# Decode attention with a squared-ReLU MLP: K transposed on VectorE in 32 by 32 blocks, scores as 16 full-width products per unit

## The chip, the cores and the metric

The kernel runs on one core of a Trainium2 chip. The metric is the device time of one execution in microseconds, 134.0 before the change (median of three runs, 133.91 to 134.0). The engines are named as in the profile: PE (TensorE), DVE (VectorE), ACT (ScalarE), POOL (GpSimd) and SP (SyncE, which here only issues transfers).

## The reference

One decode step for two batch rows of width 576: a layer norm, then an attention over the last 2048 cached positions and a two-layer MLP, both fed by the normalized row, and a sum of all three. There are 32 query heads and 16 key/value heads of 128 elements, so two query heads share one K and one V.

```python
W = min(4096, max(256, Sk // 4))                     # 2048 of 8192 positions
q = (xn @ wq).reshape(B, 1, 32, 128)
k = repeat(k_cache[:, :, Sk - W:, :], 2, axis=1)     # the same for v
p = softmax(einsum("bhqd,bhkd->bhqk", q, k) * 128 ** -0.5)
a = einsum("bhqk,bhkd->bhqd", p, v).reshape(B, 1, 4096) @ wo
h = relu(xn @ w1 + b1)
out = x + a + (h * h) @ w2 + b2                      # B = 2, w1 is 576 x 4608
```

All inputs are bfloat16. Nearly all the bytes are the K and V windows, 16.8 MB each, and the weights wq, wo, w1 and w2.

## The kernel before

**Units.** The 16 K/V heads times 2 batch rows are worked in 8 units of 4 heads of one batch row. A unit's K is one transfer of 2 MB into a tile of 128 partitions (4 heads times 32 runs of positions) by 8192 elements (64 positions of 128); V has the same form. `load_k(u)` and `load_v(u)` issue them on SP's queue; both take buffers from one pool of six. The large weights wq, w1 and wo follow each other in a single buffer (`issue_flat`), so each waits until the one before has been used up. The order of the 24 large transfers is written out by hand: k0, wq, k1, v0, k2, v1, k3, then one V and one K per unit, w1 between v5 and k7, and wo and the pieces of w2 at the end.

**The K transposes.** The scores need K with the head dimension on the partitions. `transposes(u, g)` (L258), called eight times a unit, has PE turn four 128 by 128 blocks of 4-byte pairs (two neighbouring bfloat16 elements count as one pair) into a PSUM tile `kT_ps`, and then copies that tile to `kT` in SBUF: on ACT for even g (L270), on DVE for odd g (L272).

**The scores.** `scores(u, t)` (L274) works on half a unit. Its stationary tile is a slice of `qz`, 128 by 32, with the query values of the unit's heads at their places and zeros elsewhere; four such products, one per column group of the array, run side by side, so a unit takes 16 products of 32 columns by 512. A product with `far_h` first puts a large negative number wherever row and head do not belong together. `qz` is made once, in `q_block` (L226), from the query product q_ps by way of copies (L238), transposes and copies (L254).

**The softmax.** `softmax(u)` (L288) takes the row maximum (L291) and a masked form of it (L293) on DVE, the maximum over all partitions on POOL (`partition_all_reduce`, gmax, L295), the bias on DVE (gown, L298), the exponential on ACT (L302), and turns the result in 32 by 32 blocks on DVE (pT, L305).

**The values.** `pv(u)` (L314) multiplies pT with V into o_ps, `pv_end(u)` (L326) gathers four parts into o1 on DVE, and its `fin` divides by the sum and writes the unit's columns of `ws`. pT and o1 have two buffers each, so the values of unit u-2 are worked in step u. `mlp_h` (L356) makes the hidden row; `out_acc` (L216) adds ws times wo and the hidden row times w2 into one PSUM tile.

**Order.** Matmuls and PE transposes are pinned to the order in which the program names them (`keep_in_program_order`, L93 to L97). All else is placed by a scheduler that reorders the instructions of an engine. The program runs q_block after unit 0's transposes, then one `step(u)` per unit, `mlp_h` before the last step, and the output products at the end.

Of the kernel before, what the change touches and what calls it, by code (L numbers as in the profile page):

```python
# [16 lines left out]
def kernel(  # L17
# [32 lines left out]
    JG = 8  # L50
    NG = NJ // JG
# [5 lines left out]
    TG = NG // NT  # L57
    QZ = 2 * NC
    assert SR == 32 and NG % NT == 0

# [34 lines left out]

    def transpose(*a, **k):
        tc.keep_in_program_order(nc.tensor.transpose(*a, **k))  # L97
# [18 lines left out]
    def issue_flat(w, name):  # L116
        n = w.shape[0] * w.shape[1] // P
        tl = wbig.tile([P, NH * L1], BF16, tag="wbig", name=name)
        nc.sync.dma_start(out=tl[:, 0:n], in_=w.rearrange("r n -> (r n)").rearrange("(p l) -> p l", p=P))
        return tl  # L120

    const.tile([P, 144], F32, name="pad_0")
# [15 lines left out]
    tmp_f = work.tile([P, 2, Dh], F32, tag="tmp", name="tmp_f")  # L138
# [50 lines left out]
    nc.vector.tensor_scalar(out=off[:], in0=own[:], scalar1=BIG, scalar2=-BIG, op0=ALU.mult, op1=ALU.add)  # L189
    of_h = const.tile([P, NC * WC], F32, name="of_h")  # L190
# [29 lines left out]

    qz = const.tile([P, NQ, B, 2, 3 * QZ], BF16, name="qz")
    nc.gpsimd.memset(qz[:], 0.0)
# [3 lines left out]
    def q_block():  # L226
        for t in range(NH):
            for g in range(NG4):
                o = t * LQ + g * QW
                matmul(q_ps[32 * g:32 * g + 2 * B, :], lhsT=xnT[:, t].rearrange("p x b -> p (x b)"),  # L230
                       rhs=wq_sb[:, o:o + QW], start=(t == 0), stop=(t == NH - 1), skip_group_check=True,
                       tile_position=(0, 32 * g))
        row_t = const.tile([RB, 4 * HW], BF16, tag="row", name="qrow")
        qrow = row_t[:, 0:2 * QW]
        nh = QH // 2
        for k in range(2):
            cp = nc.scalar.copy if k else nc.vector.tensor_copy
            cp(out=qrow[:, k * QW:(k + 1) * QW].rearrange("p (i a d) -> p i a d", a=2, d=Dh),  # L238
               in_=q_ps[0:RB, k * QW // 2:(k + 1) * QW // 2].rearrange("p (i d) -> p i d", d=Dh).unsqueeze(2)
               .to_broadcast([RB, nh, 2, Dh]))  # L240
        qrow_f = qrow.bitcast(F32)
        qT_ps = psum.tile([P, QH * P], F32, tag="sc", bufs=2, name="qT_ps")
        for i in range(QH):
            transpose(out=qT_ps[:, i * P:i * P + RB], in_=qrow_f[:, i * Dh:(i + 1) * Dh],
                      identity=ident_f[0:RB, 0:RB])
        qT_v = qT_ps[:].bitcast(BF16).rearrange("p (i g e x b c) -> p b x g c e i", g=NG4 // 2, e=2, x=32 // B, b=B, c=2)
        hd = Dh // 2
        for j2 in range(2):
            cp = nc.scalar.copy if j2 else nc.vector.tensor_copy
            pp = slice(hd * j2, hd * (j2 + 1))  # L250
            o = QZ + NC * j2
            for b in range(B):
                for half in range(2):
                    cp(out=qz[pp, half * NQ // 2:(half + 1) * NQ // 2, b, :, o:o + NC].rearrange(  # L254
                        "p g c (e i) -> p g c e i", e=2), in_=qT_v[pp, b, half])

    kT_tiles, sc_tiles, pT_tiles, o1_tiles, o_tiles = {}, {}, {}, {}, {}
    def transposes(u, g):  # L258
        k_f = k_tiles[u][:].bitcast(F32)
        kT_ps = psum.tile([P, JG * P], BF16, tag="kT", bufs=3, name=f"kT_ps_{u}_{g}")  # L260
        kT_f = kT_ps[:].bitcast(F32)
        for i in range(JG // 2):
            j = g * JG // 2 + i
            transpose(out=kT_f[:, i * P:(i + 1) * P], in_=k_f[:, j * P:(j + 1) * P], identity=ident_f[:])
        t, o = divmod(g, TG)
        if o == 0:
            kT_tiles[(u, t)] = ktpool.tile([P, TG * JG * P], BF16, tag="kT_sb", name=f"kT_{u}_{t}")
        kT = kT_tiles[(u, t)][:, o * JG * P:(o + 1) * JG * P]
        if g % 2 == 0:
            nc.scalar.copy(out=kT, in_=kT_ps[:])  # L270
        else:
            nc.vector.tensor_copy(out=kT, in_=kT_ps[:])  # L272

    def scores(u, t):  # L274
        tq, b = divmod(u, B)
        if t == 0:
            sc_tiles[u] = psum.tile([P, NJJ * 32], F32, tag="sc", bufs=2, name=f"sc_ps_{u}")
            matmul(sc_tiles[u][:], lhsT=far_h[:], rhs=is_h, start=True, stop=False, skip_group_check=True)
        sc_ps = sc_tiles[u]
        kT = kT_tiles.pop((u, t))[:].rearrange("p (j k c) -> p j k c", k=P, c=2)  # L280
        z = QZ * (1 - t)
        for c in range(2):
            for g in range(4):
                matmul(sc_ps[32 * g:32 * (g + 1), :], lhsT=qz[:, tq, b, c, z:z + SR],
                       rhs=kT[:, :, 32 * g:32 * (g + 1), c], start=False, stop=(t == NT - 1 and c == 1),
                       skip_group_check=True, tile_position=(0, 32 * g))

    def softmax(u):  # L288
        sc_ps = sc_tiles.pop(u)
        m1 = work.tile([P, 1], F32, tag="m1", name=f"m1_{u}")  # L290
        nc.vector.tensor_reduce(out=m1[:], in_=sc_ps[:], axis=AX.X, op=ALU.max)  # L291
        m2 = work.tile([P, NC], F32, tag="m2", name=f"m2_{u}")
        nc.vector.tensor_scalar(out=m2[:], in0=off[:], scalar1=m1[:, 0:1], scalar2=None, op0=ALU.add)  # L293
        gmax = work.tile([P, NC], F32, tag="gmax", name=f"gmax_{u}")
        nc.gpsimd.partition_all_reduce(gmax[:], m2[:], channels=P, reduce_op=ReduceOp.max)  # L295
        gown = work.tile([P, NC], F32, tag="gown", name=f"gown_{u}")
        bias = work.tile([P, 1], F32, tag="bias", name=f"bias_{u}")
        nc.vector.scalar_tensor_tensor(out=gown[:], in0=gmax[:], scalar=-scale, in1=own[:], op0=ALU.mult,  # L298
                                       op1=ALU.mult, accum_out=bias[:])
        p_sb = work.tile([P, NJJ * 32], BF16, tag="p_sb", bufs=1, name=f"p_{u}")  # L300
        o1 = keep.tile([P, Dh + 1], F32, tag="o1", name=f"o1_{u}")
        nc.scalar.activation(out=p_sb[:], in_=sc_ps[:], func=ACT.Exp, bias=bias[:, 0:1], scale=scale,  # L302
                             accum_out=o1[:, Dh:Dh + 1])
        pT = keep.tile([P, NJJ, SR], BF16, tag="pT", name=f"pT_{u}")
        nc.vector.transpose(out=pT[:].rearrange("p j r -> p (j r)"), in_=p_sb[:])  # L305
        pT_tiles[u] = pT
        o1_tiles[u] = o1
# [6 lines left out]
    def pv(u, part, parts):  # L314
        n = NJJ // parts
        if part == 0:
            o_tiles[u] = psum.tile([P, NS * Dh], F32, tag="o", name=f"o_ps_{u}")
        v = v_tiles[u][:].rearrange("p (t j s d) -> p j t s d", t=NT, s=2, d=Dh)
        for j in range(part * n, (part + 1) * n):
# [3 lines left out]
        if part == parts - 1:  # L323
            pT_tiles.pop(u)

    def pv_end(u):  # L326
# [3 lines left out]
        for k in range(NS):  # L330
            kw = dict(out=o1[:, 0:Dh], in0=o_ps[:, k * Dh:(k + 1) * Dh])
            if k == 0:
                nc.vector.tensor_scalar(scalar1=in_s[:, 0:1], scalar2=None, op0=ALU.mult, **kw)
            else:
                nc.vector.scalar_tensor_tensor(scalar=in_s[:, k:k + 1], in1=o1[:, 0:Dh], op0=ALU.mult, op1=ALU.add,  # L335
                                               **kw)

        def fin():
# [5 lines left out]
            nc.vector.reciprocal(out=linv[pp, :], in_=op[pp, Dh:Dh + 1])  # L344
            om_t = work.tile([P, Dh], F32, tag="om", name=f"om_{u}")
            om = om_t[pp, :].rearrange("p (q r) -> p q r", r=WR)
            nc.vector.scalar_tensor_tensor(out=om, in0=op[pp, 0:Dh].rearrange("p (q r) -> p q r", r=WR),
                                           scalar=linv[pp, 0:1], op0=ALU.mult, op1=ALU.mult,
                                           in1=own_c[pp, :].unsqueeze(2).to_broadcast([32, WC, WR]))
            with nc.allow_low_precision(reason="sums of one term and zeros"):  # L350
                nc.vector.tensor_reduce(out=ws[pp, :, BS * b], in_=om.rearrange("p q r -> p r q"), axis=AX.X,  # L351
                                        op=ALU.add)
# [3 lines left out]
    def mlp_h(w1_sb):  # L356
        h_ps = [psum.tile([P, HB], F32, tag="kT", bufs=3, name=f"h_ps_{k}") for k in range(2)]
# [29 lines left out]
    def step(u):  # L387
        fin = None
        w = u - 2
        with_pv = w >= 0  # L390
        for g in range(NG):
            transposes(u, g)
            if with_pv and g == 1:
                pv(w, 0, 2)
            if with_pv and g == 2:
                pv(w, 1, 2)
                fin = pv_end(w)
            if g == TG + 1:
                scores(u, 0)
            if g == TG + 2 and fin:  # L400
                fin()
        scores(u, 1)
        softmax(u)

    def pv_all(u):
        pv(u, 0, 1)
        pv_end(u)()

    for g in range(NG):
        transposes(0, g)  # L410
    q_block()
    for t in range(NT):
        scores(0, t)
    softmax(0)
    load_v(2)
    b1_rows = B_b1.rearrange("(x n) -> x n", n=HW)
# [4 lines left out]
    load_k(4)  # L421
# [16 lines left out]
    nc.sync.dma_start(out=w2a_sb[:], in_=w2_rows[0])  # L438
# [49 lines left out]
```

## Time and profile before

| What | Value |
|---|---|
| time, median of three runs | 134.0 us |
| the profiled execution's own time | 133.92 us |
| its span, first to last instruction | 132.1 us |
| PE busy | 84.6 us, 64% |
| DVE busy | 63.2 us, 48% |
| ACT busy | 46.7 us, 35% |
| POOL busy | 4.9 us, 4% |
| loads from memory | 53.6 MB, 406 GB/s over the span |
| mean granted PE clock | 0.834 |

In a line of groups stand the source line, the engine, the operation, output and inputs, shapes and the number of instructions; then the busy time and the mean of one in ns; then the engine's idle time just before them and what ended it. In a line of a timeline stand the start and the duration in us, and in brackets the idle time before. The rows PEclk and DMA have 40 digits, one for each fortieth of the span, in tenths: the granted clock of PE and the busy share of the transfer engines.

### The profile page before, as it was taken

Reading aid. Unit: us, or ns where it says so; the run is one execution under the profiler, and the core shown is the slowest. Engines: PE = TensorE matmul, PEld = TensorE weight load, DVE = VectorE, ACT = ScalarE, POOL = GpSimd, SP = SyncE. Lnnn points to the kernel's source line nnn. Section 1 sums busy time; section 2 is a strip of 40 time slices with the busy share of each in tenths; the row PEclk is TensorE's granted clock in tenths of the full one; section 3 lists DMA queues with packets and bytes.
Section 4 is the critical chain, followed back from the end, with each engine's and each line's share of the span. In section 5 each row is a group of like instructions: output and inputs, shape, how many; then the busy total and the mean of one; then the engine's idle time right before and its main releaser. Section 6 shows DMA issues by size and latency. Waiting matters only on the chain.

```text
span 132.1 us, 2285 instructions
## 1 busy us (share of the span) xinstructions
PE 84.6 (64%) x949; PEld 52.6 (40%) x949; DVE 63.2 (48%) x176; ACT 46.7 (35%) x67; POOL 4.9 (4%) x15
## 2 busy tenths in 40 slices
PE   0089319599589687697599787104819972739471
PEld 0069202286345353363455443002417640229360
DVE  7764400344557677396547687410075667550000
ACT  5725400339566085283256094200106632000000
POOL 5000000010010100100100100100000001000000
PEclk9999955959999999999779999855695999555955
DMA  4999899999999999999999999999999999899960
GB/s 160 397 437 526 369 388 442 422 432 432 429 432 422 442 417 427 437 432 437 432 427 414 437 488 402 445 424 405 427 427 442 468 435 458 376 408 418 418 255 1
DMA packets 3511, 53.76 MB, mean 407 GB/s; under 512 B 419, under 2 KB 558, under 8 KB 814
## 3 DMA queue, kind: packets, MB, share of 16 engines
q1 hardware_dynamic: 3456, 53.61, 95.2%
q8 instruction: 7, 0.11, 0.3%
q10 hardware_dynamic: 46, 0.02, 0.1%
q14 instruction: 2, 0.02, 0.0%
HBM read 53.62 MB, written 0.00 MB: 406 GB/s over the span
## 4 chain that ended last, share of the span: by engine, by line
DMA 78%; PE 15%; ACT 2%; SPq 1%; DVE 1%; issue 1%; ACTq 0%; DVEq 0%
DMA w<-in_B_w_dram 25%; DMA w2c<-in_B_w_dram 24%; DMA k<-in_A_k_cache_dram 16%; DMA wq<-in_A_wq_dram 13%; PE kT_ps L97 5%; PE h_ps L94 3%; PE q_ps L94 3%; PE sc_ps L94 2%; PE out_ps L94 1%; PE o_ps L94 1%; ACT kT L270 1%; DVE qrow L238 1%; SPq L106 0%; ACT qrow L238 0%; DVE qz L254 0%
## 5 line engine op out<-in xcount | busy, mean ns | idle before, releaser
L97 PE MATMUL kT_ps<-ident_f,k 128*128 128x128 f32 x256 | 41.4, 312 | 5.7 <-DMA k<-in_A_k_cache_dram 3.9
L97 PEld LDWEIGHTS kT_ps<-ident_f,k 128*128 128x128 f32 x256 | 32.9, 161 | 18.8 <-issue 9.9
L270 ACT COPY kT<-kT_ps 128x1024 bf16<-128x1024 bf16 x32 | 31.9, 1012 | 17.8 <-PE kT_ps L97 17.8
L272 DVE COPY kT<-kT_ps 128x1024 bf16<-128x1024 bf16 x32 | 21.8, 682 | 6.4 <-PE kT_ps L97 6.1
L94 PE MATMUL sc_ps<-kT,qz 128*32 128x512 bf16 x128 | 9.9, 388 | 6.7 <-DVE kT L272 4.7
L302 ACT ACTIVATE p<-sc_ps,bias 128x512 bf16<-128x512 f32 x8 | 5.5, 688 | 21.4 <-DVE gown L298 18.2
L94 PE MATMUL o_ps<-v,pT 128*32 128x512 bf16 x128 | 11.2, 429 | 0.0
L94 PEld LDWEIGHTS <-xnT 128*4 128x4 bf16 x108 | 3.5, 121 | 16.8 <-issue 15.2
L94 PE MATMUL h_ps<-w,xnT 128*4 128x288 bf16 x72 | 4.3, 429 | 8.0 <-DMA w<-in_B_w_dram 8.0
L305 DVE STREAM_TRANSPOSE pT<-p 128x512 bf16<-128x512 bf16 x8 | 5.7, 710 | 6.2 <-ACT p L302 6.2
L335 DVE SCALAR_TENSOR_TENSOR o<-o_ps,in_s,o 128x128 f32<-128x128 f32 x24 | 8.3, 345 | 0.4
L291 DVE TENSOR_REDUCE m<-sc_ps 128x1 f32<-128x512 f32 x8 | 5.5, 692 | 4.8 <-PE sc_ps L94 4.8
L375 DVE TENSOR_TENSOR hrow<-t 100x1152 bf16<-100x1152 f32 x2 | 2.6, 1355 | 9.6 <-ACT t L373 9.6
L94 PE MATMUL q_ps<-wq,xnT 128*4 128x512 bf16 x36 | 4.0, 627 | 4.9 <-DMA wq<-in_A_wq_dram 4.9
L295 POOL PARTITION_ALL_REDUCE gmax<-m x8 | 2.9, 367 | 104.9 <-DVE m L293 104.9
L94 PE MATMUL op_ps<-o,of_h 128*32 128x129 f32 x16 | 3.7, 316 | 4.6 <-DVE o L335 4.6
L456 ACT CAST fin_sb<-out_ps 113x144 bf16<-113x144 f32 x1 | 0.3, 280 | 17.9 <-PE out_ps L94 17.9
L94 PEld LDWEIGHTS <-qz 128*32 128x32 bf16 x128 | 2.1, 94 | 10.4 <-DVE kT L272 7.2
L97 PE MATMUL pro_ps<-ident,xn_sb 2*128 2x2 bf16 x5 | 0.9, 182 | 6.8 <-DVE xn_sb L171 6.5
L94 PEld LDWEIGHTS <-hT_sb 128*17 128x17 bf16 x144 | 3.4, 108 | 3.6 <-issue 3.5
L94 PE MATMUL out_ps<-wo,ws 128*17 128x144 bf16 x128 | 4.0, 325 | 1.2 <-DVE ws L351 1.2
L238 DVE CAST qrow<-q_ps 100x512 bf16<-100x512 f32 x1 | 0.7, 692 | 8.2 <-PE q_ps L94 8.2
(71 smaller groups left out, 57.4 us busy)
## 6 DMA issues: line engine op xcount, KB each, us to landing
k<-in_A_k_cache_dram SPq DMA_DIRECT2D x8, 2048.0 KB, 21.0
v<-in_A_v_cache_dram SPq DMA_DIRECT2D x8, 2048.0 KB, 21.5
w<-in_B_w_dram SPq DMA_DIRECT2D x1, 5184.0 KB
wq<-in_A_wq_dram SPq DMA_DIRECT2D x1, 4608.0 KB, 17.8
wo<-in_A_wo_dram SPq DMA_DIRECT2D x1, 4608.0 KB
w2a<-in_B_w_dram SPq DMA_DIRECT2D x1, 2592.0 KB, 26.9
w2b<-in_B_w_dram SPq DMA_DIRECT2D x1, 1296.0 KB
w2c<-in_B_w_dram SPq DMA_DIRECT2D x1, 864.0 KB
```

The source lines that it names most:

```text
L94: tc.keep_in_program_order(nc.tensor.matmul(*a, **k))
L97: tc.keep_in_program_order(nc.tensor.transpose(*a, **k))
L238: cp(out=qrow[:, k * QW:(k + 1) * QW].rearrange("p (i a d) -> p i a d", a=2, d=Dh), in_=q_ps[0:RB, k * QW // 2:(k + 1) * QW // 2].rearrang ...
L270: nc.scalar.copy(out=kT, in_=kT_ps[:])
L272: nc.vector.tensor_copy(out=kT, in_=kT_ps[:])
L291: nc.vector.tensor_reduce(out=m1[:], in_=sc_ps[:], axis=AX.X, op=ALU.max)
L295: nc.gpsimd.partition_all_reduce(gmax[:], m2[:], channels=P, reduce_op=ReduceOp.max)
L302: nc.scalar.activation(out=p_sb[:], in_=sc_ps[:], func=ACT.Exp, bias=bias[:, 0:1], scale=scale, accum_out=o1[:, Dh:Dh + 1])
L305: nc.vector.transpose(out=pT[:].rearrange("p j r -> p (j r)"), in_=p_sb[:])
L335: nc.vector.scalar_tensor_tensor(scalar=in_s[:, k:k + 1], in1=o1[:, 0:Dh], op0=ALU.mult, op1=ALU.add, **kw)
L375: nc.vector.tensor_tensor(out=h4[:, :, k * HB:(k + 1) * HB], in0=t4, in1=t4, op=ALU.mult)
L456: nc.scalar.copy(out=fin_sb[:], in_=out_ps[:])
```

## The change

**K's transposes go to DVE.** `transposes(u, t)`, now two calls a unit, is one DVE transpose of half a K tile, 128 by 2048 pairs, straight from the K tile to `kT`. It turns each 32 by 32 block of pairs for itself, so a block keeps its place and the four head groups of a tile stay on their own 32 partitions.

**The scores change form to fit.** The stationary tile is block-diagonal and 128 columns wide: block q holds the query values of head group q for 32 pairs of the head dimension. A unit's scores are 16 products of 128 columns by 512 (four slots of positions, two halves of the head dimension, two elements of a pair), each over the whole array, all added into the same PSUM tile.

**The stationary tiles are made per unit.** `q_block` now leaves compact queries `qc`, through copies of twice the width and eight PE transposes for four. `q_place(u)` multiplies `qc` of unit u by `own_p`, a mask of 32-row blocks, into one of two tiles `qz[u % 2]`, on POOL.

**The order changes.** `step(u)` now runs the values of unit u-2, the scores of unit u, and then the transposes of unit u+1, the second of them behind the softmax's last DVE instruction. DVE's instructions from the softmax on are pinned to program order (`dve(...)`), and so are three large loads of SP. The loads of v2 and k4 are issued before step 1. `kT_ps` is gone; the MLP's PSUM tiles get their own name. In `pv` the positions of V are numbered to match.

In the built program of the changed kernel POOL's order is: q_place(0), q_place(1), q_place(2), gmax_0, q_place(3), gmax_1, q_place(4), gmax_2 and so on to q_place(7), gmax_5, gmax_6, gmax_7. q_place(u+2) waits for PE to be done with unit u's stationary tile. The program has 13 instructions that reload POOL's code library, where the one before has 1.

```diff
@@ q_block @@
-        for k in range(2):
-            cp = nc.scalar.copy if k else nc.vector.tensor_copy
-            cp(out=qrow[:, k * QW:(k + 1) * QW].rearrange("p (i a d) -> p i a d", a=2, d=Dh),
...
+        for h in range(2):
+            cp = nc.scalar.copy if h else nc.vector.tensor_copy
+            cp(out=qrow[:, h * 2 * QW:(h + 1) * 2 * QW].rearrange("p (i a d) -> p i a d", a=NP4, d=HD),
+               in_=q_v[:, h].unsqueeze(2).to_broadcast([RB, QH, NP4, HD]))
...
+                    cp(out=qc[:, 2 * x:2 * x + 2, b, 2 * h:2 * h + 2, :].rearrange("p t e (g i) -> p t e g i", g=2),
+                       in_=qT_v[:, b, x])
+
+    def q_place(u):
+        tq, b = divmod(u, B)
+        sh = [P, NA, NP4, NC]
+        nc.gpsimd.tensor_tensor(out=qz[u % 2][:, :, QO:].rearrange("p a (q c) -> p a q c", c=32)[:, :, :, 0:NC],
+                                in0=qc[:, tq, b].unsqueeze(2).to_broadcast(sh),
+                                in1=own_p[:].unsqueeze(1).unsqueeze(3).to_broadcast(sh), op=ALU.mult)
 
-    def transposes(u, g):
-        k_f = k_tiles[u][:].bitcast(F32)
-        kT_ps = psum.tile([P, JG * P], BF16, tag="kT", bufs=3, name=f"kT_ps_{u}_{g}")
-        kT_f = kT_ps[:].bitcast(F32)
-        for i in range(JG // 2):
-            j = g * JG // 2 + i
-            transpose(out=kT_f[:, i * P:(i + 1) * P], in_=k_f[:, j * P:(j + 1) * P], identity=ident_f[:])
...
-        if g % 2 == 0:
-            nc.scalar.copy(out=kT, in_=kT_ps[:])
-        else:
-            nc.vector.tensor_copy(out=kT, in_=kT_ps[:])
+    def transposes(u, t):
+        kT = ktpool.tile([P, UE // NT], BF16, tag="kT_sb", name=f"kT_{u}_{t}")
+        n = UE // NT // 2
+        tc.keep_in_program_order(nc.vector.transpose(out=kT[:].bitcast(F32),
+                                                     in_=k_tiles[u][:].bitcast(F32)[:, t * n:(t + 1) * n]))
+        kT_tiles[(u, t)] = kT
 
     def scores(u, t):
...
-        for c in range(2):
-            for g in range(4):
-                matmul(sc_ps[32 * g:32 * (g + 1), :], lhsT=qz[:, tq, b, c, z:z + SR],
-                       rhs=kT[:, :, 32 * g:32 * (g + 1), c], start=False, stop=(t == NT - 1 and c == 1),
-                       skip_group_check=True, tile_position=(0, 32 * g))
+        for i in range(NS // NT):
+            z = QO - NC * (t * NS // NT + i)
+            for h in range(2):
+                for e in range(2):
+                    matmul(sc_ps[:], lhsT=qz[u % 2][:, 2 * h + e, z:z + P], rhs=kT[:, i, :, h, :, e], start=False,
+                           stop=(t == NT - 1 and i == NS // NT - 1 and h == 1 and e == 1), skip_group_check=True)
 
     def softmax(u):
...
         nc.gpsimd.partition_all_reduce(gmax[:], m2[:], channels=P, reduce_op=ReduceOp.max)
-        gown = work.tile([P, NC], F32, tag="gown", name=f"gown_{u}")
...
+        def rest():
+            gown = work.tile([P, NC], F32, tag="gown", name=f"gown_{u}")
+            bias = work.tile([P, 1], F32, tag="bias", name=f"bias_{u}")
+            dve(nc.vector.scalar_tensor_tensor(out=gown[:], in0=gmax[:], scalar=-scale, in1=own[:], op0=ALU.mult,
+                                               op1=ALU.mult, accum_out=bias[:]))
...
+            dve(nc.vector.transpose(out=pT[:].rearrange("p j r -> p (j r)"), in_=p_sb[:]))
...
     def step(u):
-        for g in range(NG):
-            transposes(u, g)
...
-        scores(u, 1)
-        softmax(u)
+        if w >= 0:
+            pv(w)
+        for t in range(NT):
+            scores(u, t)
+        fin = pv_end(w) if w >= 0 else None
+        rest = softmax(u)
+        if fin:
+            fin()
+        if u + 1 < NU:
+            q_place(u + 1)
+            transposes(u + 1, 0)
+        rest()
+        if u + 1 < NU:
+            transposes(u + 1, 1)
...
-    for g in range(NG):
-        transposes(0, g)
+    for t in range(NT):
+        transposes(0, t)
     q_block()
-    for t in range(NT):
-        scores(0, t)
-    softmax(0)
+    q_place(0)
+    step(0)
     load_v(2)
+    load_k(4)
...
     step(1)
-    load_k(4)
```

## The prediction

> **What bounds the kernel now.** I read the page's totals first, then the groups by form, then the queue of transfers, then POOL.
>
> ```profile
> span 132.1 us, 2285 instructions
> ...
> PE 84.6 (64%) x949; PEld 52.6 (40%) x949; DVE 63.2 (48%) x176; ACT 46.7 (35%) x67; POOL 4.9 (4%) x15
> ...
> PEclk9999955959999999999779999855695999555955
> DMA  4999899999999999999999999999999999899960
> ...
> DMA 78%; PE 15%; ACT 2%; SPq 1%; DVE 1%; issue 1%; ACTq 0%; DVEq 0%
> ```
>
> No engine is full, but the DMA row is at nine tenths from 3 to 128 us and the chain that ended last is 78% transfer. 53.6 MB at 425 GB/s take 126 us: with 2 us of start and 4 us of end that is the span. So the kernel is bound by its stream of loads as long as loads are asked for in time.
>
> ```profile
> 43.08 0.54 SPq L106 DMA_DIRECT2D k<-in_A_k_cache_dram  x1
> ...
> 61.23 0.54 SPq L106 DMA_DIRECT2D k<-in_A_k_cache_dram  x1
> ...
> 95.41 0.34 SPq L119 DMA_DIRECT2D wo<-in_A_wo_dram  x1
> ```
>
> The timeline of SP's queue: the load issued at 43.08 (k_5) is the one that PE meets at 64.3, so a load waits some 21 us behind others. Compute may lag that much before the stream runs dry. The load of wo, at 95.4, waits for the MLP's first product, since w1 and wo share a buffer.
>
> ```profile
> L97 PE MATMUL kT_ps<-ident_f,k 128*128 128x128 f32 x256 | 41.4, 312 | 5.7 <-DMA k<-in_A_k_cache_dram 3.9 <-ACT kT L270 1.8
> L270 ACT COPY kT<-kT_ps 128x1024 bf16<-128x1024 bf16 x32 | 31.9, 1012 | 17.8 <-PE kT_ps L97 17.8
> L272 DVE COPY kT<-kT_ps 128x1024 bf16<-128x1024 bf16 x32 | 21.8, 682 | 6.4 <-PE kT_ps L97 6.1
> L305 DVE STREAM_TRANSPOSE pT<-p 128x512 bf16<-128x512 bf16 x8 | 5.7, 710 | 6.2 <-ACT p L302 6.2
> L144 DVE STREAM_TRANSPOSE row<-tmp_f 128x32 f32<-128x32 f32 x1 | 0.2, 163 | 0.0
> ```
>
> The groups by form: the first three are what the change removes; the last two are the only rows of the operation it puts in their place.
>
> ```profile
> 62.66 0.69 DVE L291 TENSOR_REDUCE m<-sc_ps 128x1 f32<-128x512 f32 x1 [0.28 <-PE sc_ps L94]
> 63.38 0.23 DVE L293 TENSOR_SCALAR m<-off,m 128x8 f32<-128x8 f32 x1
> 63.78 0.37 POOL L295 PARTITION_ALL_REDUCE gmax<-m  x1 [8.82 <-DVE m L293]
> 64.18 0.17 DVE L298 SCALAR_TENSOR_TENSOR gown<-gmax,own 128x8 f32<-128x8 f32 x1 [0.57 <-POOL gmax L295]
> ...
> 64.47 0.69 ACT L302 ACTIVATE p<-sc_ps,bias 128x512 bf16<-128x512 f32 x1 [3.15 <-DVE gown L298]
> ...
> 65.28 0.71 DVE L305 STREAM_TRANSPOSE pT<-p 128x512 bf16<-128x512 bf16 x1 [0.93 <-ACT p L302]
> ```
>
> One softmax on the timeline: scores to maximum 1.0 us, POOL 0.6, and from POOL's end to pT's end 1.8. Every unit goes through POOL.
>
> ```profile
> 1.89 0.61 POOL L312 MEMSET hT_sb<- 128x612 bf16 x1
> 28.29 0.37 POOL L295 PARTITION_ALL_REDUCE gmax<-m  x1 [25.79 <-DVE m L293]
> 36.68 0.37 POOL L295 PARTITION_ALL_REDUCE gmax<-m  x1 [8.02 <-DVE m L293]
> ```
>
> POOL's timeline. Between the memset and the first reduce the built program has one instruction that leaves no row: a reload of POOL's code library (index 1, with the partition reduce). It lies in 25.8 us of idle time and cost nothing.
>
> **What goes, and what that is worth.** Gone are 256 transposes (41.4 us of PE), 32 ACT copies (31.9) and 32 DVE copies (21.8). All ran beside the stream, so this alone gains nothing: below 132 us of span the bytes hold. SP's 24 transfers keep their order; the K buffers are released by DVE in place of PE.
>
> **What comes on DVE and PE.** Two transposes of 128x2048 pairs per unit. The line through the two rows (163 ns at 32, 710 at 512) gives 163 + 2016 x 1.14 = 2.46 us. Low end 1.8 (slope of the 128x128 f32 memset, 165 ns against 59 for one element); high end 5.7 (four times 710, doubled for 4-byte elements). I take 2.46, as it is the same operation. Sixteen 128-column products per unit: four column groups side by side took 4.03/9 = 0.45 us per 512 columns in q_ps, under the halved clock, and 1.04/4 = 0.26 in o_ps at the full one; now one product has that for itself, so 4.2 to 7.2 us per unit. [...] The query block: each copy of q_ps has 1024 elements for 512, and DVE and ACT take turns there (0.69 and 0.59 become some 1.4 and 1.1); four more transposes and eight qc copies stay at about 1.4.
>
> **What comes on POOL.** q_place is an elementwise product on POOL, 128 elements: between 0.13 us (memset rate, about 1 ns an element) and 0.74 (the largest memset); I take 0.5. But the built program shows more. The scheduler puts q_place(u+2), which must wait for the last score of unit u, in front of the reduce of unit u, and sets a library reload before every change between the two kinds (index 0 for the product, 1 for the reduce): 13 reloads for 1. The order is reload, q_place(0), (1), (2), reload, gmax_0, reload, q_place(3), reload, gmax_1 and so on to gmax_5; gmax_6 and gmax_7 need none. So the reload to index 1 starts only after the scores and q_place, and the reduce, the exponent, pT and the second K transpose, which DVE holds behind gown in order, all wait for it. Behind that transpose wait the unit's last eight products and K's buffer.
>
> What does a reload, X, cost? No row has it. From below: ACT_TABLE_LOAD, 1.28 us; from above, the 25.8 us of idle POOL that held one. The nearest rows are small loads that cross this stream of transfers: the five bias loads of ACT's queue, issued from 4.43 to 5.74 us, whose data moves at 8.65, 11.44, 14.33, 17.10 and 18.56 in the packet records: 4.2 to 12.8 us after issue, mean 8.9. [...]
>
> [...]
>
> **The sum.** S(u) is the end of unit u's scores. S(0): q_ps ends at 23.27; + 1.4 + 1.1 (copies) + 1.4 (transposes, qc) + 0.5 (q_place) + 7.2 = 34.9. gmax_0 ends at 34.9 + 0.5 + X + 0.6 = 44.9.
> From one reduce to the next there are two paths, which meet in q_place. DVE and PE: 1.8 (to pT) + 2.46 + 0.1 + 3.6 (eight products) = 8.0. POOL's reload to index 0, X = 8.9. The longer one counts; then 0.5 + 8.9 + 0.6: a period of 18.9 us. Five periods: gmax_5 at 139.4, S(6) = 147.4. In the trace of before unit 6 was there at 82.8.
> The rest, from S(6): the w1 products end at +4.8 (w1 has long landed); kT_7's first half, relu, exp 6, the first half of hrow and pT_6 to +7.5; kT_7's second half +10.0; hrow +11.3; its transposes (1.72) +13.1; pv(5) +14.5; scores of unit 7 +22.1; softmax (1.0 + 0.6 + 1.8) +25.5; then as in before's timeline pv_end(6) 1.5 and the 5.8 us to the last ws: +32.8; output products 4.02 + 1.5 + 1.26 + 1.34: +41; last copy and store +43.8. The wo load, asked for at +4.8, needs 23.6 us for its 10 MB and the w2 behind it: hidden. Span 191.2; the profiled execution took 133.92 for a span of 132.1, so + 1.8: **193 us**. That execution stands 0.1 below the median of 134.0.
> With X = 4.2 the period is 8.0 + 0.5 + 4.2 + 0.6 = 13.3 and the time 160; with 12.8 it is 26.7 and 236.
>
> **Rivals.** (1) The reload is cheap, PE is slow. Up to X = 3.4 it fits beside DVE's maximum, the previous unit's end and the first transpose (1.0 + 1.0 + 2.46, less 0.5 + 0.6). Then DVE and PE set the period: 3.6 + 1.0 + 1.0 + 2.46 + 1.8 + 2.6 = 12.5 us (11.5 in the first two steps) against 9.9 for two loads: S(6) at 107.9, 153 us. For it: ACT's load takes 1.28. [...]
> (2) The other side: POOL's wait is hidden and the units keep up, so the stream stays the bound: 134 us, no change. It decides at a period of 9.7 us (S(6) at 93, where the tail is ready with the last w2c). That needs X under 3.4 and also full clock, transposes below 2.3. For it: clock row 10 tenths in most of 30 to 84 us. Against: at 2.46 and full clock the period is still 11.0 and the time 137, and the 13 reloads.
> (3) The reload is dearer, 13 us to 25.8: 238 to 370 us. Nothing in the trace excludes it.
>
> **How the numbers follow.** Forecast (X from 4.2 to 12.8) 0.82; rival 1 0.06; rival 2 0.04; rival 3 0.08. The range is the forecast's own, cut a little at the dear end: 160 to 230. A measurement here tells a change from 0.2% on; rival 2 splits evenly between the same and faster: faster 0.02, same 0.03, slower 0.95.
>
> **What would show it.** Right: POOL's reduces stand 15 to 25 us apart for units 1 to 5 and about 8 to 12 between 5 and 6; DVE's gown waits on POOL for many microseconds; the DMA row has holes from 50 us on; the new transposes near 2.5 us and the products 0.45 apart. Wrong: reduces 10 us apart, DMA still at nine tenths (rivals 1, 2). I would be wrong in size if reloads are much faster while the stream is idle, for then the mean of five loads under full load is too high.

## The result, and the profile after

The changed kernel takes 186.3 us (median of four executions, 184.1 to 186.8) against 134.0 us for the kernel before beside it (133.9 to 134.2): a ratio of 1.387, with a 95% interval from 1.375 to 1.399. The execution that was profiled took 186.83 us, 184.9 of them span. Here and below, executions more than 1.5% above the fastest of their kernel are left out of its ratio.

The first view is the page of the changed kernel: its totals, the two rows by fortieths of the span, and the shares of the chain that ended last.

```profile
span 184.9 us, 1756 instructions
...
PE 86.9 (47%) x697; PEld 35.2 (19%) x697; DVE 80.0 (43%) x161; ACT 15.8 (9%) x35; POOL 8.6 (5%) x24
...
PEclk9999999855576855885768586755755795597569
DMA  5999999999399408940999989914700079899500
...
DVE 30%; PE 28%; issue 24%; DMA 10%; ACT 4%; POOL 2%; SPq 0%; ACTq 0%; POOLq 0%
```

ACT's work fell from 46.7 to 15.8 us and no engine is over half full, yet the kernel is 52 us longer. The row of transfers, at nine tenths from end to end before, is now full of holes from the eleventh digit (46 us) on. The chain's share of transfers went from 78% to 10%. In its place stand DVE, PE, and 24% of "issue", which is 45 us in which the chain shows no work at all.

The second view is the groups by form of the changed kernel (after the bar: busy us, mean ns of one; then the idle time ahead of the group and what ended it).

```profile
L94 PE MATMUL sc_ps<-kT,qz 128*128 128x512 bf16 x128 | 52.4, 583 | 60.5 <-DVE kT L271 60.2 <-POOL qz L263 0.3
L271 DVE STREAM_TRANSPOSE kT<-k 128x2048 f32<-128x2048 f32 x16 | 36.5, 2284 | 0.1
...
L263 POOL TENSOR_TENSOR qz<-qc,own_p 128x128 bf16<-128x128 bf16 x8 | 3.1, 397 | 73.2 <-PE sc_ps L94 37.6 <-ACT qc L257 24.7 <-issue 10.9
L295 POOL PARTITION_ALL_REDUCE gmax<-m x8 | 3.1, 386 | 83.4 <-issue 55.8 <-DVE m L293 27.6
...
L300 DVE SCALAR_TENSOR_TENSOR gown<-gmax,own 128x8 f32<-128x8 f32 x8 | 1.3, 162 | 42.5 <-POOL gmax L295 42.5
```

DVE sits idle for 42.5 us in front of eight small instructions, all of it waiting for gmax, and PE for 60.2 us in front of the scores, ended by K's transposes, of which DVE holds each unit's second one behind gown. POOL's reduces are as short as before, 0.39 us, but ahead of them POOL itself was idle for 55.8 us with no releaser: no semaphore ended that time. The timeline of POOL shows where.

```profile
54.29 0.39 POOL L263 TENSOR_TENSOR qz<-qc,own_p 128x128 bf16<-128x128 bf16 x1 [8.42 <-PE sc_ps L94]
64.59 0.39 POOL L295 PARTITION_ALL_REDUCE gmax<-m  x1 [9.91 <-issue]
...
110.52 0.39 POOL L263 TENSOR_TENSOR qz<-qc,own_p 128x128 bf16<-128x128 bf16 x1 [10.86 <-issue]
121.58 0.39 POOL L295 PARTITION_ALL_REDUCE gmax<-m  x1 [10.67 <-issue]
...
146.22 0.37 POOL L295 PARTITION_ALL_REDUCE gmax<-m  x1 [8.84 <-DVE m L293]
```

Between a q_place and the reduce behind it POOL stands idle for 9.9 and 10.7 us and names nobody; the last reduce shown, which follows another reduce and so needs no reload, waits for DVE's m like every reduce before the change. One unit on the chain that ended last reads so (start, duration, work):

```profile
53.35 0.70 DVE m L291
54.08 0.23 DVE m L293
54.31 2.22 DVE kT L271
56.54 8.05 issue
64.59 0.40 POOL gmax L295
65.02 0.18 DVE gown L300 x2
...
65.29 0.79 ACT p L304 x2
66.10 0.71 DVE pT L307
66.81 2.21 DVE kT L271
...
69.06 3.59 PE sc_ps L94 x8
```

The maximum and the first K transpose run beside POOL's gap; then the chain has nothing to run for 8.05 us; then gmax, the exponent, pT, the second K transpose and the last eight products follow one after the other. K's buffer comes free only behind that second transpose: SP issues the load of k5 at 69.03 us, where it stood at 43.08 before, and that of wo at 148.18 where it stood at 95.41. That is how holes come into the stream. From the timeline of SP's queue:

```profile
69.03 0.54 SPq L108 DMA_DIRECT2D k<-in_A_k_cache_dram  x1
...
148.18 0.34 SPq L121 DMA_DIRECT2D wo<-in_A_wo_dram  x1
```

### The profile page after: what moved, and what is told of

Its sections match the earlier page's. It is cut to its first block, busy times and chain, and to the rows that moved or that the text cites. A ratio compares the mean times of both kernels' runs of the same rounds, so it can differ in the third digit from the quotient of the medians.

```text
span 184.9 us, 1756 instructions
## 1 busy us (share of the span) xinstructions
PE 86.9 (47%) x697; PEld 35.2 (19%) x697; DVE 80.0 (43%) x161; ACT 15.8 (9%) x35; POOL 8.6 (5%) x24
## 4 chain that ended last, share of the span: by engine, by line
DVE 30%; PE 28%; issue 24%; DMA 10%; ACT 4%; POOL 2%; SPq 0%; ACTq 0%; POOLq 0%
PE sc_ps L94 18%; DVE kT L271 16%; DMA wq<-in_A_wq_dram 10%; PE out_ps L94 3%; DVE m L291 3%; DVE pT L307 3%; ACT p L304 3%; PE q_ps L94 2%; PE o_ps L94 2%; DVE ws L352 1%; DVE hrow L376 1%; DVE om L348 1%; POOL gmax L295 1%; DVE o L336 1%; DVE m L293 1%
## 5 line engine op out<-in xcount | busy, mean ns | idle before, releaser
L94 PE MATMUL sc_ps<-kT,qz 128*128 128x512 bf16 x128 | 52.4, 583 | 60.5 <-DVE kT L271 60.2
L271 DVE STREAM_TRANSPOSE kT<-k 128x2048 f32<-128x2048 f32 x16 | 36.5, 2284 | 0.1
L94 PEld LDWEIGHTS <-qz 128*128 128x128 bf16 x128 | 16.7, 132 | 92.6 <-issue 89.9
L300 DVE SCALAR_TENSOR_TENSOR gown<-gmax,own 128x8 f32<-128x8 f32 x8 | 1.3, 162 | 42.5 <-POOL gmax L295 42.5
L94 PE MATMUL o_ps<-v,pT 128*32 128x512 bf16 x128 | 13.4, 501 | 0.0
L94 PE MATMUL q_ps<-wq,xnT 128*4 128x512 bf16 x36 | 4.0, 627 | 12.2 <-DMA wq<-in_A_wq_dram 12.2
L295 POOL PARTITION_ALL_REDUCE gmax<-m x8 | 3.1, 386 | 83.4 <-issue 55.8
L263 POOL TENSOR_TENSOR qz<-qc,own_p 128x128 bf16<-128x128 bf16 x8 | 3.1, 397 | 73.2 <-PE sc_ps L94 37.6
L94 PEld LDWEIGHTS <-pT 128*32 128x32 bf16 x128 | 4.8, 118 | 3.6 <-issue 2.0
L99 PE MATMUL hp<-ident,hrow 100*128 100x100 bf16 x18 | 1.7, 287 | 6.7 <-DVE hrow L376 6.7
L94 PEld LDWEIGHTS <-ws 128*17 128x17 bf16 x128 | 3.7, 137 | 1.5 <-DVE ws L352 1.5
L94 PEld LDWEIGHTS op_ps<-o,of_h 128*32 128x32 f32 x16 | 1.4, 137 | 12.0 <-issue 12.0
L94 PE MATMUL sc_ps<-ident,far_h 4*128 4x512 bf16 x8 | 3.5, 440 | 0.0
```

The lines of the kernel that those rows point to most:

```text
L94: tc.keep_in_program_order(nc.tensor.matmul(*a, **k))
L263: nc.gpsimd.tensor_tensor(out=qz[u % 2][:, :, QO:].rearrange("p a (q c) -> p a q c", c=32)[:, :, :, 0:NC], in0=qc[:, tq, b].unsqueeze(2).t ...
L271: tc.keep_in_program_order(nc.vector.transpose(out=kT[:].bitcast(F32), in_=k_tiles[u][:].bitcast(F32)[:, t * n:(t + 1) * n]))
```

## The experiments

The theory: the 13 reloads of POOL's code library make the time, since one lies between the scores and the reduce in six units. (The order of POOL's work in the trace has twelve places that need one, the first product and eleven changes between the two kinds behind it; where the thirteenth stands, no trace shows.) The rival: the DVE transposes, the full-width products and their order make most of it, and the reload little.

### q_place on DVE: the changed kernel with one reload

```diff
-        nc.gpsimd.tensor_tensor(out=qz[u % 2]...,
+        dve(nc.vector.tensor_tensor(out=qz[u % 2]...,
                                 ..., op=ALU.mult)
```

> The changed kernel with q_place on DVE, pinned in its program order, and nothing else moved: POOL then has one reload, before its first reduce. Theory (the reloads between product and reduce are what costs): the step falls from some 19 us to the chain of DVE and PE, which the trace of the changed kernel gives as 3.6 + 1.0 + 1.0 + 2.3 + 1.8 + 2.2 and about 0.3 for the product, 12 us at the halved clock and some 10.5 at the full one; unit 6's scores end at 95 to 104 us and the time is 136 to 147 us. Rival A (the full-width products and DVE's transposes set the pace, POOL merely waits for them): 180 us or more, little changed. Rival B (the product itself is slow, wherever it stands): 175 to 185.

Measured: 135.4 us (median of four, 134.5 to 138.5) beside 134.0 for the kernel before, a ratio of 1.0053 (1.0033 to 1.0074). This one edit takes 51.0 of the 52.3 us away, a little more than the 136 to 147 us expected: unit 6's scores ended at 92.2 us. From its page:

```profile
PE 74.7 (56%) x697; PEld 32.6 (24%) x697; DVE 81.2 (61%) x169; ACT 15.8 (12%) x35; POOL 5.3 (4%) x16
...
PEclk9999999999999779779769869869995559955599
DMA  4999899999999999999999999989999999999910
...
DVE 43%; PE 30%; DMA 13%; ACT 6%; issue 5%; SPq 0%; ACTq 0%
```

The holes in the stream are gone and the chain's "issue" fell from 24% to 5%. One unit of its chain:

```profile
61.51 0.70 DVE m L291
...
63.29 0.19 DVE qz L263
63.48 2.22 DVE kT L271
65.70 0.07 DVE gown L300 x2
...
65.88 0.79 ACT p L304 x2
66.69 0.71 DVE pT L307
67.40 2.20 DVE kT L271
...
69.64 1.92 PE sc_ps L94 x8
```

The reduce of this unit, on POOL's timeline:

```profile
62.63 0.37 POOL L295 PARTITION_ALL_REDUCE gmax<-m  x1 [9.70 <-DVE linv L345]
```

It now hides beside DVE's own work, here the end of the unit before, and a unit takes 9.2 to 10.3 us from reduce to reduce, close to the 9.8 us that two loads of 2 MB need at the 427 GB/s measured in the kernel before between 3 and 128 us. Set beside the changed kernel, the 51.1 us between the two spans come out in three pieces. The first reduce starts 11.4 us earlier (34.08 against 45.48). The five periods behind it last 49.0 against 91.5 us, 42.5 less: the chain's "issue" there was 33.2 us, and 8.2 us are the eight last products of each unit, at 1.9 instead of 3.5 to 3.6 us; 1.1 us is left. From the sixth reduce to the end it takes 2.8 us longer. So most of the loss is the wait itself, and part is the pace at which PE ran: over the eight last products of these units the granted clock was 0.50 to 0.54 in the changed kernel; here the slices of PEclk in which they end read 9.

### All of q_place ahead of the units: two reloads

The eight products are made on POOL right behind q_block, into eight stationary tiles that lie where w2c's pieces come later (so those loads wait for the scores of the last unit).

```diff
-    q_place(0)
+    for u in range(NU):
+        q_place(u)
...
-            q_place(u + 1)
```

> The changed kernel with all eight products of q_place on POOL directly after the query block, into eight stationary tiles (kept where the last piece of w2 lies later); one reload then stands between them and the first reduce, and none after. Theory: one wait of about 5 us at unit 0, then steps of 10.5 to 12 us, 139 to 152 us in all, although POOL does the same products as in the changed kernel. Rival A: 180 or more. Rival B (POOL's product is what costs): as the changed kernel, less the one or two products that stood on the path, 180 or more.

Measured: 143.2 us in the median, the four times between 139.8 and 145.1, too far apart for a ratio, but all more than 38 us below the changed kernel. From the timeline of POOL in this kernel (its profiled execution took 144.2 us):

```profile
27.36 2.90 POOL L263 TENSOR_TENSOR qz_all<-qc,own_p 128x128 bf16<-128x128 bf16 x8 [21.28 <-ACT qc L257]
41.21 0.39 POOL L295 PARTITION_ALL_REDUCE gmax<-m  x1 [10.95 <-issue]
50.07 0.36 POOL L295 PARTITION_ALL_REDUCE gmax<-m  x1 [8.47 <-DVE m L293]
```

The product and its tiles are POOL's as in the changed kernel, and all but one of the bare waits are gone: POOL may do the work, as long as it does not change back and forth. The one that remains, 10.95 us, sets the first reduce 7.1 us later than with q_place on DVE (41.21 against 34.08); 4.71 us of it stand bare on the chain, for the 5 expected. The late pieces of w2, asked for at 121.6 us, are mixed into the rest, so the remaining gap to 134 was not divided.

### The reloads alone, in the kernel before

One product of 128 by 128, which nobody reads, is pinned on POOL in front of each reduce of the kernel before. That makes 16 reloads of its 1 and leaves the rest as it is (the product's tile takes the room of 64 floats of padding).

```diff
+        tc.keep_in_program_order(nc.gpsimd.tensor_tensor(out=idle_t[:], in0=ident[:], in1=ident[:], op=ALU.mult))
-        nc.gpsimd.partition_all_reduce(gmax[:], m2[:], channels=P, reduce_op=ReduceOp.max)
+        tc.keep_in_program_order(nc.gpsimd.partition_all_reduce(gmax[:], m2[:], channels=P, reduce_op=ReduceOp.max))
```

> The kernel before, with one product of 128x128 elements on POOL, read by nobody, in front of each reduce; the scores, the transposes and the loads are as before. Theory: two reloads stand between two reduces, so the reduces are 16 to 20 us apart where they were 9 to 11, the last at about 150 us, and the time is 165 to 190 us. Rivals A and B (PE, DVE or the product): POOL has 9 us of idle time per unit, so the product of 0.4 us is hidden and the time stays at 134 to 135.

Measured: 186.6 and 191.0 us in two executions; the shorter, which is the profiled one, is 52.7 above the kernel before. Its row of transfers on the page, and its POOL on the timeline:

```profile
DMA  5989999999996999609999999100499998000000
```

```profile
42.04 0.39 POOL L296 TENSOR_TENSOR idle_t<-ident 128x128 bf16<-128x128 bf16 x1 [11.51 <-issue]
52.89 0.39 POOL L297 PARTITION_ALL_REDUCE gmax<-m  x1 [10.46 <-issue]
```

With PE's transposes, the ACT and DVE copies and the four-column products all as they were, POOL's changes of code alone give the same picture: 0.4 us of work between gaps of 5.7 to 11.8 us, the eight reduces 13.8 to 22.8 us apart (16 to 20 were expected, and the last at 150 where it came at 167), holes in the stream. The DVE transposes are not needed for the loss.

### The price of a change of code, by itself

In two small kernels POOL alternates eight products and eight reduces, without loads in the first and with 28 loads of 2 MB on SP's queue in the second.

```diff
+    for n in range(28):      # only in the second
+        nc.sync.dma_start(out=tl[:], in_=cache[...])
+    for n in range(8):
+        tc.keep_in_program_order(nc.gpsimd.tensor_tensor(out=b_t[:], in0=a_t[:], in1=a_t[:], op=ALU.mult))
+        tc.keep_in_program_order(nc.gpsimd.partition_all_reduce(g_t[:], m_t[:], channels=P, reduce_op=ReduceOp.max))
```

> Nothing of the computation: POOL alternates eight products of 128x128 with eight reduces, with one reload before each, and no load runs beside them. Theory: 6 to 8 us for each reload, so the reduces are 13 to 17 us apart. Rival (a reload is about as dear as ACT's table load, 1.3 us): 3 to 4 us apart.

> As the kernel in which POOL alternates product and reduce and nothing else is computed, but with 28 loads of 2 MB running beside it through the six buffers. Theory (a reload fetches code through the memory that the loads use): the idle time before each POOL instruction grows from 5.7 to 7.6 us to some 9 to 11.5. Rival (the longer reloads of the changed kernel come from something else, such as DVE's transposes holding POOL up): it stays at 6 to 7.5 us.

Measured without loads (113.6 us in all), POOL's timeline:

```profile
21.52 0.39 POOL L103 TENSOR_TENSOR b_t<-a_t 128x128 bf16<-128x128 bf16 x1 [7.27 <-issue]
27.86 0.40 POOL L104 PARTITION_ALL_REDUCE g_t<-m_t  x1 [5.95 <-issue]
```

Measured with loads (166.6 us in all), the same view:

```profile
32.44 0.39 POOL L103 TENSOR_TENSOR b_t<-a_t 128x128 bf16<-128x128 bf16 x1 [12.06 <-issue]
43.13 0.39 POOL L104 PARTITION_ALL_REDUCE g_t<-m_t  x1 [10.30 <-issue]
...
156.76 0.39 POOL L103 TENSOR_TENSOR b_t<-a_t 128x128 bf16<-128x128 bf16 x1 [7.11 <-issue]
163.14 0.40 POOL L104 PARTITION_ALL_REDUCE g_t<-m_t  x1 [5.99 <-issue]
```

In the kernel without loads the gap ahead of a reduce is 5.7 to 6.0 us and ahead of a product 6.7 to 7.6. While the loads run at some 420 GB/s it is 8.3 to 10.4 and, after the first, 11.0 to 12.1. The last pair of the second kernel, behind its last load, is back at these prices, 7.1 and 6.0 us. So the price depends on whether loads run beside it, and it is the change of code that costs, not the two instructions (0.4 us each). DVE's busy time is 0.00 us in each window read in these two kernels (65.0 to 72.8, 82.4 to 90.2 and 99.7 to 110.5 us in both, and five gaps of the second), so its transposes are not what holds POOL up. How the code reaches POOL is not shown: in the kernel without loads the transfers move 0 GB/s in those three windows, in which the changes go on.

### The end of the kernel, in another order

The chain of the kernel with q_place on DVE ends on DVE and PE, not on a load. This kernel is that one with the hidden row's products pinned behind the transposes of unit 7, and the rest of `mlp_h` (turning the hidden row) behind the last step.

```diff
+            dve(nc.vector.tensor_tensor(out=h4[...], in0=t4, in1=t4, op=ALU.mult))
+        return hrow
+
+    def mlp_t(hrow):
...
     step(NU - 1)
+    mlp_t(hrow)
```

> The kernel with q_place on DVE, with DVE's two hrow products pinned behind unit 7's transposes and the turning of the hidden row moved behind unit 7's scores. Theory: what is left of the loss without the reloads (135.4 against 134.0) lies in the chain after unit 6, where unit 7's first transpose stands 2.6 us behind the hrow products; ws is then ready at about 120 us in place of 122.5, the last load decides again and the time is 133.8 to 134.5. Rival: the rest lies in the steps before (10.3 us for a unit against 9.9 for its loads), and the time stays at 135 to 136.

Measured: 134.3 us (median of twelve, 134.1 to 135.9) beside 134.1 for the kernel before, a ratio of 1.0043 (1.0015 to 1.0070). Nine of the twelve lie from 134.1 to 134.8, three from 135.3 to 135.9. The end of the chain in the profiled execution (134.18 us, span 132.1 as before the change):

```profile
75.42 25.43 DMA v<-in_A_v_cache_dram
...
100.86 28.19 DMA w2c<-in_B_w_dram
...
129.38 0.28 ACT fin_sb L459
```

In that execution the stream is the bound again, as in the kernel before, and no version with DVE transposes came out below it. The interval overlaps that of the previous order, so that the new end is worth anything is not shown; what the three longer times spend is open.

## Why the prediction was right, point by point

**The bound, and the worth of what goes: right.** With 73.3 us of ACT and PE work and 21.8 us of DVE copies gone, and DVE's transposes (36.5 us) and wider products in their place, the changed kernel without its reloads ends at 1.0053 of the time before. Beside a full stream the removal gained nothing.

**A reload per change of code, and X: right in kind, near in size.** I took 8.9 us from the five small bias loads that crossed the stream; that a reload goes the way of such a load no run shows. Ahead of the six reduces that needed it POOL stood idle for 11.0, 9.9, 8.8, 8.6, 10.7 and 6.8 us, 9.3 in the mean. That a mean of small loads on another engine's queue comes so near is in part luck: in the kernel without loads, with nothing to cross, the same wait is still 5.7 to 6.0 us ahead of a reduce and 6.7 to 7.6 ahead of a product, idle time without a releaser. In the changed kernel the price ahead of a reduce is half as much again in the mean, 9.3 us against 5.9 there. The guard that I set up, that reloads may be faster while the stream is idle, was the right one. The windows of the changed kernel between a reduce and the product behind it show it (from and to, length, then each engine's busy time, and at the end the granted clock, the busy share of the transfers and GB/s):

```profile
65.00:72.80 7.80, 3.74 (x13) 1.16 (x16) 4.49 (x9) 0.78 (x2) 0.01 (x1) 0.50 0.36 134
82.40:90.20 7.80, 3.73 (x13) 1.17 (x16) 4.48 (x9) 0.78 (x2) 0.00 (x0) 0.59 0.35 134
99.70:110.50 10.80, 5.27 (x27) 1.81 (x27) 7.33 (x14) 0.78 (x2) 0.00 (x0) 0.68 1.02 430
```

Where the transfers were a third busy, the reload was done within 7.8 us, before the scores; where they were full it took 10.8 and came last.

**"The longer one counts; POOL's reload to index 0": the step that failed.** I let that reload set the first part of the period, 8.9 us against 8.0 of DVE and PE. In four of the five steps q_place waited last for PE's scores, some 7.8 to 8.4 us after the reduce; the reload set it only once, at 110.52. The kernel's own slowness made the holes in which the reload is cheap. The period came out at 18.3 us in the mean (15.4 to 22.3) for the 18.9 forecast: 8.55 to the product for 8.9, 0.40 for 0.5, 8.96 to the reduce for 8.9, and 0.39 for 0.6. That the wrong branch cost so little is luck: the two paths lay 0.9 us apart in the forecast, and the one that decided came out at 7.8 to 8.4 us for its 8.0.

**The transposes and the products: right.** 2.28 us for 2.46 (the line through two far smaller ones held to 8%), 3.59 us for eight products against 3.6 (granted 0.50 to 0.54 in those stretches). The sum takes 0.45 us a product, the pace of q_ps under the halved clock; that idle time of PE brings that clock on no run shows: in the changed kernel PE idled for 12.2 us before q_ps, with 1.00 granted there and in q_ps. The scores of unit 0 took 5.9 us for 7.2 and ended at 33.9 for 34.9: the first eleven products start 0.43 us apart and the last five 0.22, with the granted clock at 1.00 all through. So the 0.45 us that I read off q_ps is not explained by the granted clock alone: q_ps takes 4.01 us in the kernel before, at 0.50, and 4.01 us in the changed one, at 1.00. q_place took 0.40 us for 0.5.

**The end: mis-sized by 4 us.** From S(6) to the end I summed 43.8 us; it took 39.8 (145.1 to 184.9). The hidden row and the transposes beside it were done 1.6 us early, the last scores took 5.8 us where I had 7.6 with what lies ahead of them, and the output products 6.35 us for 8.1; smaller terms ran about 1.2 us longer. With S(6) 2.3 us early that is the 6.3 us between the forecast span of 191.2 and the measured 184.9. The load of wo was hidden, as forecast.

**The rivals.** The cheap reload with a slow PE (153 us) falls twice over: the reload costs 9.3 us, and the kernel that really has no reloads in its units took 135.4, since its eight products ran at 1.92 us. They do not always: in the kernel with the other end two early units took 3.6 us for eight, where 0.73 was granted in the mean (30 to 60 us), and the execution still ended at 134.2. The hidden wait (134 us) is close to what the kernel does without the reloads. I had that period as 11.0 us at full clock, and it is 9.2 to 10.3: each term is a little smaller, the two transposes above all (2.2 us for 2.46 and 2.6). The dear reload (13 us and more) did not occur; the longest was 12.1. (By the forecast's own sum its far end, 25.8 us, gives 379 us and not 370.)

## What to carry to other kernels

Read the order that a scheduler gives each queue, also of an engine that is 4% busy, and count the changes between kinds of code on POOL: one between scores and softmax in six units, with the changes back between them, cost 52 us; the same work on DVE cost 1.4 us, and all of it ahead of the loop 6 to 11 us, late loads of w2 included. On these profiles such a change was idle time without a releaser, 5.7 to 12.1 us of it, ahead of instructions of 0.4 us; look for it wherever "issue" has a large share of the chain. Work taken off engines that ran beside a full stream bought nothing here, and the wait that came with the change held up the loads and went into the time.

## What the runs showed of the hardware that was not expected

The price of a change of POOL's code differs with its direction: 7.1 us in the mean to the product and 5.9 to the reduce without loads, 11.0 to 12.1 and 8.3 to 10.4 under loads. So a stream of some 420 GB/s adds 2.4 to 5 us to it, and the price is back at 7.1 and 6.0 us behind the last load.

The wait acts back on its own price: it holds K's buffers, which leaves the transfers a third busy, and the reload in that stretch is done in under 7.8 us where it took 10.9 beside full queues. PE's granted clock between 30 and 60 us was 0.66 in the changed kernel, 0.73 in the kernel before with reloads put in, and 0.89 and 0.73 in the two kernels with q_place on DVE: whether the waits lower it, these runs do not settle. Nor does the granted clock alone give PE's pace: of unit 0's scores in the changed kernel the first eleven products start 0.43 us apart and the last five 0.22, with 1.00 granted throughout.
